# Six block numbers for each tile in one register load, and new durations for the queue planner, in a block-sparse attention and feed-forward kernel

## The chip, the cores and the metric

The kernel runs on one core of a Trainium2 chip. The metric is the time of one execution on the device, in microseconds (us); smaller is better. A core has TensorE (PE in the profile, its weight loads PEld), VectorE (DVE), ScalarE (ACT), GpSimd (POOL) and SyncE (SP), each with an instruction queue of its own that is worked off in order. All DMAs of this kernel are issued from SP's queue.

## The reference, cut to what matters

```python
# q, k, v: (4, 8, 768, 64); sampled_blocks: (24, 3); blocks of 32 positions
scores = scale * np.matmul(q, k.transpose(0, 1, 3, 2))
mask = np.abs(blk_i - blk_j) <= 1                      # the window
mask = mask | (blk_i == 0) | (blk_j == 0) | (blk_i == n_blocks - 1) | (blk_j == n_blocks - 1)
for qb in range(n_blocks):
    for kb in sampled_blocks[qb]:                      # three sampled blocks for each block row
        mask[qb*32:(qb+1)*32, kb*32:(kb+1)*32] = True
attn = softmax(np.where(mask, scores, -1e9))
x = np.matmul(attn, v).transpose(0, 2, 1, 3).reshape(3072, 512)
h = x @ w_in                                           # 512 -> 2048
return np.maximum(0.01 * h, h) @ w_out                 # 2048 -> 512
```

The sampled block numbers are an input, so the kernel learns only on the chip which blocks of K and V to fetch.

## The kernel before, in words

**Tiles.** A tile is two block rows (64 queries) of all eight heads of one of four batches. There are twelve tiles in a batch. Tile 0 holds the first and the last block row, which see all keys. The other eleven, T = 1 to 11, so 44 in all, see twelve blocks of keys, called slots: slots 0 to 3 are the window, 4 and 5 the first and last block, and 6 to 11 are the six sampled ones, three for each of the tile's two block rows. Each value is kept as two halves of 16 bits, so that matmuls run in f16.

**Gathering K.** `gather_k` fills one of two buffers `kg` with the twelve key blocks from the transposed keys `kt`: VectorE copies the window (and the edges once for a batch), and GpSimd copies the six sampled blocks, one copy each, in two tasks of three. **Gathering V.** `gather_v` fills one of two buffers `vg` by DMA from a scratch array `scr` in DRAM: one 128-row load for the window, two edge loads once for a batch and buffer, and six 32-row loads (moves) of sampled blocks, again in two tasks of three. A buffer of either kind comes free when the matmuls of the tile two before have read it.

**Block numbers.** `build_masks` clamps the sampled numbers, multiplies them by 32 and leaves them in the SBUF tile `offs`. `sampled_of` (line 982 of the profile) loads them into registers of the engine that needs them: GpSimd for the copies of K (line 1005), SP for the moves of V (line 1036). A call loads the three numbers of one half-task, so there are two calls for each tile on each of the two engines.

**After the gathers.** Scores (`s`) are matmuls of `kg` with the stacked queries `qs` and their half-swapped twin `qxs`; VectorE and ScalarE make the softmax (`p`, then the two halves `pp`); SP transposes `pp` into `pt` by DMA (in the first item, TensorE does); `pair_av` multiplies `pt` with `vg` in three chunks of four slots, in the order of the slots, so the last three sampled blocks are in its last chunk. Four tiles make an item; each item goes through the feed-forward layer (`h`, then `ht` and `g`, then `o`), whose matmuls are TensorE's other work. Weights are decoded, scaled and split during the first quarter of the run.

**What sets the order.** Every call on an engine is recorded as a task of a `Plan` (so most instructions have line 384 in the profile). `Plan.order` then runs a simulation with the durations of `cost`: each engine takes, among the tasks whose inputs are ready, the one of the lowest priority number, which follows the step (half a head pair of a tile) at which it was recorded or which it serves. TensorE also prefers to stay with matmuls of one kind. The order in which tasks begin in that simulation is the fixed order in which each engine's instructions are written. A task has `busy` (how long its engine is taken), `late` (when its result is there) and, for a DMA, `loads`: the transfers, which fly 1.25 us, share the DMA engines and are done 0.4 us after they were served. A task of SP with `loads` is only done, for tasks that need it, when its last load has landed. The half-tasks of the gathers do not go through `cost`; their durations are given where they are recorded:

```python
plan.task("POOL", copies, 2150.0, 2150.0, cells(kt) | cells(offs), cells(kg[:, :, at:at + NR * BLOCK]))
...
plan.task("SP", moves, 1850.0, 1850.0, cells(scr[b]) | cells(offs), into, "",
          [BLOCK * (9.3 + 0.055 * 2048) / 16] * NR)
```

The last arguments but the loads are what the task reads and writes, as sets of cells; a task that writes a cell comes after the one that wrote or read it before.

Of the kernel before, what the change touches and what calls it, by code (L numbers as in the profile page):

```python
# [16 lines left out]
I32 = mybir.dt.int32  # L17
# [15 lines left out]
    "ahead": 3,  # L33
    "av_lag": 3,
    "bs": 1500,
    "early": 2,
    "flag": 1,
    "g": 2,
    "g_at": 0,
# [348 lines left out]
def cost(eng, method, a, k):  # L388

    out = k.get("out", a[0] if a else None)  # L390
    n = elements(out)
    apply = lambda x: hasattr(x, "ap")
    if eng == "PE":
        lhs, rhs = a[1], a[2]
        cols = elements(rhs)
        if lhs.dtype == F32:
            return 60.0 + 4 * cols, 300.0 + 4 * cols, "f", []
        half = elements(lhs) <= 64
        t = (cols / 2.4 + 2.5) / CFG["clock"]
        return (t / 2 if half else t), t + 180, ("a" if half else "f"), []  # L400
    if eng == "SP" or method.startswith("dma"):
        turned = method == "dma_start_transpose"
        w = transfer(k["out"], k["in_"], turned)
        rows = len([d for d in list(k["out"].ap) if d[1] > 1])
        busy = 1050.0 + 0.37 * n if turned else 380.0 + 110 * max(0, rows - 1)
        return busy, busy, "", [w]
    if eng == "DVE":
        ptr = sum(1 for x in (k.get("scalar"), k.get("scalar1"), k.get("scale")) if apply(x)) > 0
        src = [x for m, x in k.items() if m in ("in0", "in1", "in_") and apply(x)]
        wide = [x for x in src if elements(x) > 1]  # L410
        f = 1.0
        if method in ("tensor_copy", "tensor_scalar") and len(wide) == 1 and wide[0].space == bass.MemoryType.SB:
            f = 0.5
            if method == "tensor_copy" and wide[0].dtype == F16 and out.dtype == F16:
                f = 0.25
        if method == "tensor_reduce":
            n = elements(k["in_"])
        d = 145 + 62 * ptr + n * f / 0.96
        if len(wide) == 2 and all(x.space == bass.MemoryType.SB for x in wide) and n >= 256:
            d *= 1.08  # L420
        acc = method == "tensor_tensor_reduce"
        return max(d - 70, 60.0), d + 12 + 80 * acc, "", []
    if eng == "ACT":
        src = a[1]
        ptr = any(apply(k.get(x)) for x in ("scale", "bias"))
        d = n * 0.833 + (155 if src.space == bass.MemoryType.PSUM else 187) + 93 * ptr
        acc = "accum_out" in k
        return d - 92 + 100 * acc, d + 14 + 93 * acc, "", []
    d = 120 + n * (2.2 if method == "tensor_tensor" else 1.3)
    return d + 20, d + 12, "", []  # L430
# [3 lines left out]
def tile_block_sparse_attention_ffn(  # L434
# [165 lines left out]
    iota = cst.tile([NB, NB], F32, name="iota")  # L600
    tmps = pf.tile([P, DM], F32, tag="ob", name="tmps", bufs=CFG["ob"])
    sb = tmps[:NB, :2 * NR].bitcast(I32)
    row = tmps[:1, 6:6 + 2 * NB * NR].bitcast(I32)
    eq = tmps[:NB, 150:150 + NR * NB].rearrange("p (r b) -> p r b", r=NR)
    sels = [tmps[:NB, 222 + P * a:222 + P * (a + 1)].rearrange("p (a b c) -> p a b c", a=2, b=2) for a in range(2)]
    assert 222 + 2 * P <= DM and 6 + 2 * NB * NR <= 150
    offs = cst.tile([1, NT - 1, 2, 4], I32, name="offs")
    mask = cst.tile([P, NT - 1, SLOTS], F32, name="mask")

    def load_constants():  # L610
        nc.sync.dma_start(out=eye, in_=c_eye)
        nc.vector.tensor_copy(out=eye16, in_=eye)
        nc.sync.dma_start(out=row, in_=sampled.bitcast(I32).rearrange("(o a) b -> o (a b)", o=1))
        nc.sync.dma_start(out=allow, in_=c_allow)
        nc.sync.dma_start(out=iota, in_=c_iota)
        nc.sync.dma_start(out=sb, in_=sampled.bitcast(I32))

    def build_masks():
        blocks = row.rearrange("p (a b) -> p a b", b=2)[:, NR:NR + (NT - 1) * 2 * NR, 0]
        nc.vector.memset(offs, 0)  # L620
        nc.vector.tensor_scalar(
            out=offs[:, :, :, :NR], in0=blocks.rearrange("p (t a r) -> p t a r", a=2, r=NR), scalar1=0, scalar2=NB - 1,
            op0=ALU.max, op1=ALU.min)
        nc.vector.tensor_scalar(out=offs, in0=offs, scalar1=5, scalar2=None, op0=ALU.logical_shift_left)
        sf = cst.tile([NB, NR], F32, name="sf")
        nc.vector.tensor_copy(out=sf, in_=sb.rearrange("p (a b) -> p a b", b=2)[:, :, 0])

        ok = cst.tile([NB, NR], F32, name="ok")
        hit = cst.tile([NB, NB], F32, name="hit")
        for r in range(NR):  # L630
            nc.vector.tensor_scalar(out=eq[:, r, :], in0=iota, scalar1=sf[:, r:r + 1], scalar2=None, op0=ALU.is_equal)
            nc.vector.tensor_tensor(out=hit, in0=eq[:, r, :], in1=allow, op=ALU.mult)
            nc.vector.tensor_reduce(out=ok[:, r:r + 1], in_=hit, op=ALU.add, axis=AX.X)
            nc.vector.tensor_tensor(out=allow, in0=allow, in1=eq[:, r, :], op=ALU.max)
        nc.vector.tensor_scalar(out=ok, in0=ok, scalar1=-1.0, scalar2=1.0, op0=ALU.mult, op1=ALU.add)

        at = cst.tile([NB, NT - 1, 2, NR], F32, name="at")
        nc.gpsimd.affine_select(
            out=at.rearrange("p t a r -> p (t a) r"), in_=ok.unsqueeze(1).to_broadcast([NB, NB - 2, NR]),
            pattern=[[-1, NB - 2], [0, NR]], base=-1, channel_multiplier=1,  # L640
            compare_op=ALU.is_equal, fill=0.0)
        pm = corner()[:, :(NT - 1) * 2 * NR].rearrange("p (t a r) -> p t a r", t=NT - 1, a=2)
        for a in range(2):
            sel = sels[a]
            nc.vector.memset(sel, 0.0)
            nc.vector.memset(sel[:, :, a, :], 1.0)
            nc.tensor.matmul(
                pm[:, :, a, :], sel.rearrange("p a b c -> p (a b c)"), at[:, :, a, :], start=True, stop=True)
        nc.vector.tensor_scalar(
            out=mask[:, :, 6:], in0=pm.rearrange("p t a r -> p t (a r)"), scalar1=-1.0, scalar2=-NEG,  # L650
            op0=ALU.add, op1=ALU.mult)
        nc.vector.memset(mask[:, :, :6], 0.0)
        for hh in range(2):
            a, b = (slice(D * hh + BLOCK * i, D * hh + BLOCK * (i + 1)) for i in range(2))
            nc.vector.memset(mask[a, :, 3:4], NEG)
            nc.vector.memset(mask[b, :, 0:1], NEG)
            nc.vector.memset(mask[a, 0:1, 4:5], NEG)
            nc.vector.memset(mask[b, NT - 2:NT - 1, 5:6], NEG)
# [318 lines left out]
    kgs, vgs = {}, {}  # L977
    last_use = {}

    def sampled_of(T, a, engine):  # L980

        _, rows = tc.nc.values_load_multi_w_load_instructions(
            offs.ap[:1, T - 1, a, :NR], engines={engine}, min_val=0, max_val=S - BLOCK,
            skip_runtime_bounds_check_because="the block numbers are clamped to the sequence before they are shifted")
        return zip(range(6 + a * NR, 6 + (a + 1) * NR), rows)

    kgb = [pa.tile([P, H, KEYS], F16, tag=f"kg{i}", name=f"kg{i}", bufs=1) for i in range(2)]
    ends = {}
# [1 line left out]
    def gather_k(b, T):  # L990
# [6 lines left out]
        if ends.get(n) != b:  # L997
            ends[n] = b
            nc.vector.tensor_copy(
                out=kg[:, :, P:P + Q2].rearrange("p h (n l) -> p h n l", l=BLOCK),  # L1000
                in_=kt.rearrange("p h (n l) -> p h n l", l=BLOCK)[:, :, 0:NB:NB - 1, :])
        for a in range(2):
            def copies(a=a):
                for slot, off in sampled_of(T, a, mybir.EngineType.Pool):
                    tc.nc.gpsimd.tensor_copy(  # L1005
                        out=kg.ap[:, :, slot * BLOCK:(slot + 1) * BLOCK], in_=kt.ap[:, :, bass.ds(off, BLOCK)])
            at = (6 + a * NR) * BLOCK
            plan.task("POOL", copies, 2150.0, 2150.0, cells(kt) | cells(offs), cells(kg[:, :, at:at + NR * BLOCK]))
            yield
        em = pa.tile([P, KEYS], BF16, tag="em", name=f"em_{b}_{T}", bufs=2)  # L1010
        nc.gpsimd.tensor_copy(
# [8 lines left out]
    def gather_v(b, T):  # L1020
# [6 lines left out]
        if vends.get(n) != b:  # L1027
            vends[n] = b
            for slot, a in ((4, 0), (5, S - BLOCK)):
                ps, c = place(slot)  # L1030
                nc.sync.dma_start(out=vg[ps, c, :], in_=scr[b][a:a + BLOCK, :])
        for a in range(2):
            def moves(a=a):
                for slot, off in sampled_of(T, a, mybir.EngineType.SP):
                    ps, c = place(slot)
                    tc.nc.sync.dma_start(out=vg.ap[ps, c, :], in_=scr[b].ap[bass.ds(off, BLOCK), :])
            into = set()
            for slot in range(6 + a * NR, 6 + (a + 1) * NR):
                ps, c = place(slot)
                into |= cells(vg[ps, c, :])  # L1040
            plan.task("SP", moves, 1850.0, 1850.0, cells(scr[b]) | cells(offs), into, "",
                      [BLOCK * (9.3 + 0.055 * 2048) / 16] * NR)
        vgs[b, T] = vg.rearrange("p c (h x) -> p c h x", h=H)

# [578 lines left out]
```

## Time and profile before

| | |
|---|---|
| median of three runs | 924.11 us (923.51 to 927.22) |
| the profiled execution: its time, its span | 927.57 us, 925.9 us |
| granted TensorE clock, mean over the span | 0.932 |
| busy: PE, DVE, ACT, POOL | 767.3, 626.3, 509.4, 330.0 us |
| instructions | 20826 |

Busy time is the time in which an engine worked on something; instructions of a queue itself (register loads, DMA issues, waits) are not counted in it and carry a q after the engine's name, as in SPq. A row of the list of waits says who was idle, for whom, how long in total, how many times, and the longest of these. A row of the view of one line or tile gives the count, then the least, median and greatest duration in ns.

### The profile page before, as it was taken

The numbers are of one execution on the slowest core, as the hardware profiler recorded it, in microseconds if no ns is written. First come the engines' busy times: TensorE is split into PE (matmuls) and PEld (weight loads), VectorE is DVE, ScalarE is ACT, GpSimd is POOL, SyncE is SP. The second block draws the span as 40 slices with busy tenths as digits, with TensorE's granted clock in tenths as the row PEclk, the third lists the DMA queues.
The fourth block names the chain that finished last, engine by engine and source line by source line (L and its number), as shares of the span: only waits on it lengthen the run. The fifth ranks groups of instructions, "written<-read, shape, count | busy, mean of one in ns | idle before, by whom it ended". The sixth has DMA issues, their size and how long they took to land. (4 is left out here: it accounts for less than half of the span.)

```text
span 925.9 us, 20826 instructions
## 1 busy us (share of the span) xinstructions
PE 767.3 (83%) x7204; PEld 499.0 (54%) x7204; DVE 626.3 (68%) x1650; ACT 509.4 (55%) x1087; POOL 330.0 (36%) x469
## 2 busy tenths in 40 slices
PE   2647566688889978988788988988898899999998
PEld 2425443444556645555554655655565555656664
DVE  4698789998979945856748657667467466474221
ACT  5678766556655635645546556556357355274121
POOL 0234356523324523433413433324314344242221
PEclk9566678888999999999999999999999999999999
DMA  9504896488797767798677878786765867466000
GB/s 182 201 18 124 256 237 171 115 197 166 149 169 168 169 133 153 155 175 160 138 169 132 169 148 161 177 155 138 166 146 123 161 125 156 89 133 125 1 23 24
DMA packets 312231, 133.29 MB, mean 144 GB/s; under 512 B 275005, under 2 KB 287294, under 8 KB 312126
## 3 DMA queue, kind: packets, MB, share of 16 engines
q1 hardware_dynamic: 312126, 131.96, 65.7%
q8 instruction: 57, 0.93, 0.4%
q14 instruction: 48, 0.39, 0.1%
HBM read 65.57 MB, written 12.58 MB: 84 GB/s over the span
## 5 line engine op out<-in xcount | busy, mean ns | idle before, releaser
L384 PEld LDWEIGHTS <-W 128*128 128x128 f16 (+1 forms) x2480 | 237.8, 101 | 83.6 <-DVE W L384 24.5
L384 PE MATMUL o<-W,g 128*128 128x512 f16 x1152 | 278.1, 388 | 4.0 <-DVE g L384 2.8
L384 PE MATMUL h<-x,W 128*128 128x256 f16 x2304 | 278.4, 276 | 3.0 <-ACT x L384 2.1
L384 POOL TENSOR_TENSOR g<-ht,g 128x512 f16<-128x512 f32 x96 | 117.1, 1220 | 285.0 <-DVE g L384 207.0
L384 PEld LDWEIGHTS <-g 128*128 128x128 f16 x1152 | 109.6, 100 | 132.5 <-issue 21.0
L384 DVE SCALAR_TENSOR_TENSOR pp<-p,r,pp 128x384 f16<-128x384 f32 x208 | 147.6, 738 | 45.6 <-ACT pp L384 45.1
L384 ACT ACTIVATE p<-p,mx 128x384 f32<-128x384 f32 x208 | 125.8, 606 | 91.9 <-DVE mx L384 91.2
L1005 POOL COPY kg<-kt 128x256 f16 x264 | 125.9, 515 | 138.5 <-PE s L384 113.7
L384 ACT ACTIVATE pp<-p,r 128x384 f16<-128x384 f32 x208 | 118.8, 606 | 75.4 <-DMA pt<-pp 26.8
L384 PE MATMUL av<-pt,vg 128*64 128x128 f16 x2112 | 90.5, 228 | 54.5 <-DMA vg<-scr 29.6
L384 DVE SCALAR_TENSOR_TENSOR ht<-h,gd,ht 128x512 f32<-128x512 f32 x80 | 59.9, 749 | 106.3 <-ACT ht L384 105.8
L384 DVE CUSTOM_DVE_ANT_0 p<-s,em,nsc 128x384 f32<-128x384 f32 x176 | 104.7, 609 | 31.6 <-PE s L384 30.6
L384 ACT ACTIVATE ht<-h,gs 128x512 f32<-128x512 f32 x80 | 54.5, 681 | 118.4 <-PE h L384 110.7
L384 PEld LDWEIGHTS <-vg 128*64 128x64 f16 x2112 | 71.8, 114 | 88.4 <-issue 70.2
L384 PE MATMUL s<-kg,qs 128*64 128x384 f16 x352 | 64.0, 354 | 15.9 <-DVE mx L384 14.0
L384 POOL TENSOR_TENSOR x<-xf,x 128x256 f16<-128x256 f32 x48 | 35.9, 747 | 96.2 <-ACT x L384 96.0
L384 PE MATMUL s<-kg,qxs 128*64 128x384 f16 x352 | 63.5, 349 | 4.7 <-DMA qxs<-qs 4.7
L384 PEld LDWEIGHTS <-qs 128*64 128x64 f16 x416 | 29.2, 114 | 40.9 <-issue 32.0
L384 DVE CAST g<-ht 128x512 f16<-128x512 f32 x96 | 42.5, 443 | 10.8 <-PE o L384 6.5
L384 ACT ACTIVATION_READ_ACCUMULATOR p<-p,mx 128x1 f32 x208 | 39.1, 188 | 0.0
L384 DVE TENSOR_SCALAR sum<-sum 128x2 f32<-128x2 f32 x96 | 28.5, 297 | 15.3 <-ACT p L384 14.7
L384 POOL TENSOR_TENSOR W<-W 128x1024 f16<-128x1024 f32 x12 | 28.1, 2349 | 27.9 <-ACT W L384 25.6
(117 smaller groups left out, 759.8 us busy)
## 6 DMA issues: line engine op xcount, KB each, us to landing
vg<-scr SPq DMA_DIRECT2D x280, 64.0 KB, 1.9
vg<-scr SPq DMA_DIRECT2D x44, 256.0 KB, 3.2
v<-in_v_dram SPq DMA_DIRECT2D x32, 192.0 KB, 4.2
qxs<-qs SPq DMA_DIRECT2D x48, 128.0 KB, 2.4
scr<-v SPq DMA_DIRECT2D x16, 384.0 KB, 3.3
rq<-in_q_dram SPq DMA_DIRECT2D x20, 256.0 KB, 3.9
W<-in_moe_w_in_dram SPq DMA_DIRECT2D x5, 1024.0 KB, 7.5
out_dram<-ob SPq DMA_DIRECT2D x20, 256.0 KB, 2.5
```

What stands on the lines that cost most here:

```text
L384: self.plan.task(self.eng, lambda: f(*a, **k), busy, late, reads, writes, kind, loads)
L1005: tc.nc.gpsimd.tensor_copy(out=kg.ap[:, :, slot * BLOCK:(slot + 1) * BLOCK], in_=kt.ap[:, :, bass.ds(off, BLOCK)])
```

## The change

One load of six numbers takes the place of two loads of three: the first half-task of a tile's gather loads all six registers of its engine, and the second uses the last three of them. `offs` holds eight words for a tile in one row instead of two rows of four. So that the registers are not overwritten in between, the half-tasks of K write a made-up cell `("registers",)` and those of V a made-up cell `("moves",)`, which puts all half-tasks of one kind in one chain, across tiles too.

The planner's durations change as well. A half-task of K was 2150 ns; it is now 560 for each of three copies, and 800 more in the first half for the load. A half-task of V was 1850 ns; it is now 560 for each of three moves, and 800 more in the first half. Every other DMA that is not a transpose is planned at 425 ns for its issue, and 110 more for each dimension beyond the first, where it was 380.

```diff
-    "early": 2,
+    "kcopy": 560.0, "load": 800.0, "vmove": 560.0, "early": 2,
...
-        busy = 1050.0 + 0.37 * n if turned else 380.0 + 110 * max(0, rows - 1)
+        busy = 1050.0 + 0.37 * n if turned else 425.0 + 110 * max(0, rows - 1)
...
-    offs = cst.tile([1, NT - 1, 2, 4], I32, name="offs")
+    offs = cst.tile([1, NT - 1, 8], I32, name="offs")
...
-    def sampled_of(T, a, engine):
+    def sampled_of(T, engine):
...
-            offs.ap[:1, T - 1, a, :NR], engines={engine}, min_val=0, max_val=S - BLOCK,
+            offs.ap[:1, T - 1, :2 * NR], engines={engine}, min_val=0, max_val=S - BLOCK,
...
-        return zip(range(6 + a * NR, 6 + (a + 1) * NR), rows)
+        return list(zip(range(6, SLOTS), rows))
...
+        found = []
         for a in range(2):
             def copies(a=a):
-                for slot, off in sampled_of(T, a, mybir.EngineType.Pool):
+                if not a:
+                    found.extend(sampled_of(T, mybir.EngineType.Pool))
+                for slot, off in found[a * NR:(a + 1) * NR]:
...
-            plan.task("POOL", copies, 2150.0, 2150.0, cells(kt) | cells(offs), cells(kg[:, :, at:at + NR * BLOCK]))
+            t = CFG["kcopy"] * NR + (0.0 if a else CFG["load"])
+            plan.task("POOL", copies, t, t, cells(kt) | cells(offs),
+                      cells(kg[:, :, at:at + NR * BLOCK]) | {("registers",)})
...
+        got = []
         for a in range(2):
             def moves(a=a):
-                for slot, off in sampled_of(T, a, mybir.EngineType.SP):
+                if not a:
+                    got.extend(sampled_of(T, mybir.EngineType.SP))
+                for slot, off in got[a * NR:(a + 1) * NR]:
...
-            into = set()
+            into = {("moves",)}
...
-            plan.task("SP", moves, 1850.0, 1850.0, cells(scr[b]) | cells(offs), into, "",
+            t = CFG["vmove"] * NR + (0.0 if a else CFG["load"])
+            plan.task("SP", moves, t, t, cells(scr[b]) | cells(offs), into, "",
                       [BLOCK * (9.3 + 0.055 * 2048) / 16] * NR)
```

More of the change, by code (lines that the diff above doesn't have):

```diff
@@ L602, in tile_block_sparse_attention_ffn @@
     sb = tmps[:NB, :2 * NR].bitcast(I32)
-    row = tmps[:1, 6:6 + 2 * NB * NR].bitcast(I32)
+    rows = tmps[:1, 6:6 + 2 * NB * NR].bitcast(I32)
     eq = tmps[:NB, 150:150 + NR * NB].rearrange("p (r b) -> p r b", r=NR)
@@ L612, in load_constants @@
         nc.vector.tensor_copy(out=eye16, in_=eye)
-        nc.sync.dma_start(out=row, in_=sampled.bitcast(I32).rearrange("(o a) b -> o (a b)", o=1))
+        nc.sync.dma_start(out=rows, in_=sampled.bitcast(I32).rearrange("(o a) b -> o (a b)", o=1))
         nc.sync.dma_start(out=allow, in_=c_allow)
@@ L618, in build_masks @@
     def build_masks():
-        blocks = row.rearrange("p (a b) -> p a b", b=2)[:, NR:NR + (NT - 1) * 2 * NR, 0]
+        of_tile = rows.rearrange("p (a b) -> p a b", b=2)[:, NR:NR + (NT - 1) * 2 * NR, 0].rearrange(
+            "p (t a) -> p t a", a=2 * NR)
         nc.vector.memset(offs, 0)
         nc.vector.tensor_scalar(
-            out=offs[:, :, :, :NR], in0=blocks.rearrange("p (t a r) -> p t a r", a=2, r=NR), scalar1=0, scalar2=NB - 1,
-            op0=ALU.max, op1=ALU.min)
+            out=offs[:, :, :2 * NR], in0=of_tile[:1], scalar1=0, scalar2=NB - 1, op0=ALU.max, op1=ALU.min)
         nc.vector.tensor_scalar(out=offs, in0=offs, scalar1=5, scalar2=None, op0=ALU.logical_shift_left)
```

## The prediction

> **What bounds the kernel now.** I read the page's busy times first, then the stages by windows, TensorE's waits in the stage that has most of them, and last SP's queue around one gather. TensorE is the busiest engine by far, and its clock is nearly full after the first quarter:
>
> ```profile
> PE 767.3 (83%) x7204; PEld 499.0 (54%) x7204; DVE 626.3 (68%) x1650; ACT 509.4 (55%) x1087; POOL 330.0 (36%) x469
> PEclk9566678888999999999999999999999999999999
> ```
>
> By stages (time in the window, then each engine's busy time and count, the granted clock, the DMA engines' share):
>
> ```profile
> core 0: us, PE busy (x) PEld busy (x) DVE busy (x) ACT busy (x) POOL busy (x), PEclk, DMA share, GB/s
> 0.00:85.00 85.00, 43.81 (x360) 30.91 (x360) 59.96 (x193) 59.25 (x107) 18.63 (x32) 0.70 0.50 126
> 85.00:250.00 165.00, 121.47 (x1130) 79.82 (x1130) 148.72 (x353) 108.82 (x211) 76.21 (x84) 0.81 0.74 185
> 700.00:850.00 150.00, 138.52 (x1384) 89.88 (x1381) 90.95 (x240) 77.39 (x181) 59.10 (x91) 0.99 0.64 132
> 250.00:700.00 450.00, 391.60 (x3811) 250.33 (x3812) 309.19 (x837) 250.14 (x572) 159.81 (x250) 0.99 0.77 157
> ```
>
> The last row is a window of its own for the middle of the run. TensorE idles 41 us in the first 85, 44 us up to 250, 58.4 us from 250 to 700 (450 less 391.60), and 11.5 us from 700 to 850. Up to 250 VectorE is the limit (148.72 of 165 busy: weights are prepared there), and no gather is on the path. In the middle stage these are the waits, against the only large one of the stage from 700 to 850 (last row, of a second answer):
>
> ```profile
> PE av L384 <- DMA vg<-scr: 29.6, 20, 2.7
> PE av L384 <- DMA pt<-pp: 14.0, 17, 1.7
> PE s L384 <- DMA qxs<-qs: 4.4, 4, 1.4
> PE s L384 <- DVE mx L384: 4.1, 5, 2.2
> ...
> PE av L384 <- DMA pt<-pp: 10.4, 10, 2.3
> ```
>
> Half of TensorE's idle time in the middle, 29.6 of 58.4 us, is `av` waiting for V's gather: 20 waits of 1.48 us in the mean, all of these before 700. The rest is mostly transposes that SP issues too. So what SP issues for V and when, and where the plan puts `av` against it, is where this change can act. One wait seen close, SP's rows and then TensorE's (start, length, count; a register load has no row of its own here, and fills the time ahead of the L1036 rows):
>
> ```profile
> 565.98 0.49 SPq L384 DMA_DIRECT2D vg<-scr  x1
> 567.46 1.45 SPq L1036 DMA_DIRECT2D vg<-scr  x3
> 569.01 1.26 SPq L384 DMA_TRANSPOSE pt<-pp  x1
> 571.60 1.34 SPq L1036 DMA_DIRECT2D vg<-scr  x3
> ...
> 572.69 0.41 PE L384 MATMUL av<-pt,vg 128*64 128x128 f16 x8
> 574.43 0.64 PE L384 MATMUL av<-pt,vg 128*64 128x128 f16 x16 [1.33 <-DMA vg<-scr]
> ```
>
> Eight matmuls, two chunks of slots, run; the third chunk is the last three blocks, issued until 572.94, and TensorE waits 1.33 us for them. TensorE's place for `av` was fixed by the plan, which had V there sooner.
>
> **The change part by part.** *The loads themselves.* These rows have the register loads of both queues, what SP does for one move (three rows of L1036), and the other DMAs in play:
>
> ```profile
> L982 POOLq TENSOR_LOAD <-offs x88: 724/740/2223, 26.6 to 820.3; - x88
> L982 SPq TENSOR_LOAD <-offs x88: 664/690/1141, 83.5 to 845.2; - x88
> L1036 SPq FUSED_REGOPS  x147: 37/37/47, 250.2 to 694.8; - x147
> L1036 SPq MOVE vg<-scr x147: 29/29/38, 250.2 to 694.9; - x147
> L1036 SPq DMA_DIRECT2D vg<-scr x147: 315/316/1650, 250.3 to 695.0; - x147
> DMA to landing us min/median/max: 1.7/1.8/3.6
> L384 SPq DMA_DIRECT2D vg<-scr x60: 332/526/1662, 82.1 to 842.1; - x60
> L384 SPq DMA_DIRECT2D qxs<-qs x48: 467/582/1060, 18.6 to 819.3; - x48
> L384 SPq DMA_TRANSPOSE pt<-pp x188: 1209/1238/3180, 127.5 to 853.6; - x188
> ```
>
> Each queue loses 44 of its 88 loads, and each of the other 44 fetches six numbers. No row shows a load of six. If it costs what one of three costs, 0.690 us, SP saves 0.690 for each tile, 30 us of queue time in all; if it goes by the number of values, 1.380 us, it saves nothing. I take 1.34: a queue step that touches no memory takes 0.037 (FUSED_REGOPS), so 0.653 of the 0.690 is fetching, far above any such step, which looks more like three trips of 0.218 than like one; 0.037 + 6 x 0.218 = 1.34. The saving is then 2 x 0.690 - 1.34 = 0.04 us for each tile, under 2 us in 44 tiles: nothing.
> The Trainium skill, page "Runtime: NRT & Kernel Launch", section "Instruction fetch mechanics", speaks against the change here: it states that a register load costs about 200 ns for each register, even for many at once. By that page three would be 0.6 us, which the trace's 0.690 does not contradict, and six an estimated 1.29 (0.69 + 0.6), a saving of 0.09 us for each tile and 4 us of SP's queue in all; no run here has another count to try it on.
>
> *What the plan thinks of V.* This is the term I count on. With both halves back to back the gather looks like this:
>
> ```profile
> 445.00 1.66 SPq L384 DMA_DIRECT2D vg<-scr  x1
> 447.65 3.60 SPq L1036 DMA_DIRECT2D vg<-scr  x6
> 451.35 1.25 SPq L384 DMA_TRANSPOSE pt<-pp  x1
> ```
>
> From the end of the window's load (446.66) to the last move's end (451.25) are 4.59 us, both register loads included; the plan had 2 x 1.85 = 3.70, so V is 0.89 us later than planned, before anything that lands late. After the change it is 4.59 less 2 x 0.69 plus 1.34, so 4.55, and the plan has 2.48 + 1.68 = 4.16: 0.39 late. The plan gets 0.50 us nearer (with a load at 0.690, 3.90 against 4.16: 1.15 us nearer; at 1.380, 0.46 nearer). The fixed order then puts `av` that much later against V, and TensorE does `h` or `o` in between: 20 waits x 0.50 = 10 us of the 29.6.
> Not all is kept, for the transposes are late next. With no wait for V, the stage from 700 to 850 has 10.4 us of waits for `pt` in 150, so 31 in 450, where the middle stage has 14.0: had all 29.6 gone, 17 would come back and 42% be kept. By its whole idle time, 11.5 in 150 or 34.5 in 450 against 58.4, 24 of 29.6 or 81% would be kept. Between them I take 60%: 6 us. The ends are 0 (all comes back) and 24 us (the middle as good as the stage after it).
>
> *The chain of half-tasks.* In the plan V's second half now starts only after the first has landed, so something else of SP's queue goes between. Often that is so already (the transpose between the two halves at 569.01), and a transpose of 1.24 us is one that the plan knows and prices. I count nothing for it, between minus 1.24 us in a tile whose halves lay together (the second half is late by a transpose) and some gain (the plan delays `av` as well). It is the place of the slow rival below. Across tiles the chain adds nothing: the tile before has landed long ago.
>
> *K.* On GpSimd 0.74 becomes at most 1.48 ahead of the first three copies, and nothing ahead of the second. I cost that at nothing, since the queue fetches registers while the engine waits for the buffer, and since `s` waits for no copy of K in the middle stage:
>
> ```profile
> POOL kg L1005 <- PE s L384: 113.7, 30, 8.8
> PE o L384 <- POOL g L384: 1.0, 2, 0.7
> ```
>
> Were that cover gone, 44 x 0.74 = 33 us of GpSimd would lie ahead of K and of what is queued behind it, the splits `g` and `x`; `o` waits for `g` 1.0 us in the whole run, and GpSimd is busy 159.81 of 450. In the plan a tile's K goes from 4.30 to 4.16, hardly a move.
>
> *Other DMAs.* 425 for 380, and 110 for a second dimension: 0.535 where it was 0.490, against 0.526 and 0.582 in the rows above. Nothing gets faster; the order may change anywhere, from the first load on, and by the rows I can give that no sign. In `build_masks` the same instructions run on as many words: nothing.
>
> *Sum.* 6 us from V, the rest nothing. Against the profiled execution (927.57 us, its span 925.9 and 1.7 around it) that is 921.6; that execution lies 3.5 above the median of 924.11, so against the median 918.
>
> **The rivals.** *First, the load is one trip.* At 0.690 SP's queue gets 0.690 us for each tile and V's lateness falls by 1.15 us: 20 x 1.15 = 23 us, 60% of it 14: 910. For it: the numbers lie side by side in one row. Against it: 0.690 is long for one trip beside the 0.037 of a register step.
>
> *Second, all comes back.* The plan's nearer V moves `av` later, but `av` then waits for `pt`, or SP's order, shuffled by the 45 ns on each DMA, loses elsewhere what it wins here. For it: `pt` waits 10.4 us in the one stage without waits for V. It gives 924. That the change does little (a load by values, K hidden) is in here too.
>
> *Third, slower: V's second half caught behind a blocked step.* SP works in order. If what goes between the halves is a step that itself must wait, the second half sits behind it. How long such steps wait in the middle stage:
>
> ```profile
> SPq L384 <- PE s L384: 28.3, 31, 2.4
> SPq L384 <- PE av L384: 21.8, 23, 2.2
> ```
>
> The mean is 0.91 and 0.95. With 147 / 6 = 24 tiles in the stage, 24 x 0.93 = 22 us that the plan doesn't see, 60% of it 13, less the 6 won: 931. It decides once half the tiles (12 x 0.93 x 0.6 = 6.7) are hit. For it: every tile now has such a gap, and the last chunk, which waits, is the one behind it. Against it: many tiles have the gap now, and the step between is mostly a transpose.
>
> **How the numbers follow.** A difference under 0.5%, 4.6 us here, can't be told from no change. Chances: the forecast 0.36 (918, its own range 911 to 923), the load in one trip 0.20 (910, down to 900 with the 24 us of the upper end), all back 0.20 (924), slower 0.24 (931, up to 937 without the 6 won). The range of 904 to 933 leaves out about one in ten on each side. Faster by over 0.5%, below 919.5: 0.32 of the forecast's 0.36 and all of the first rival's 0.20, so 0.52; slower, above 928.7: the third rival's 0.24; within: 0.24.
>
> **What would show it.** Register loads at 44 on each queue; their median near 1.3 us, not 0.7. Waits of `av` for `vg` in the middle fall from 29.6 to about 20 us, at most 1 us each in most cases, and those for `pt` rise from 14. K shows no wait of `s` on GpSimd. I am wrong if the load's median is 0.7 (then it should be near 910), if the waits for `vg` stay or grow (the third rival, with SP's waits between the two halves), or if the idle time before 250 changes by more than a few us, which none of these terms explains.

## The result, and the profile after

The changed kernel took 889.39 us (median of four, 885.38 to 891.25) against 924.79 us of the kernel before beside it: a ratio of 0.9609, 95% interval 0.9568 to 0.9649. That is 3.9% faster, 35 us, where 918 was forecast and 904 was the low end.

The profiled execution took 888.39 us, its span 886.7. The page's lines of the span and of the busy times, then four stages by windows (columns as before):

```profile
span 886.7 us, 20717 instructions
PE 761.0 (86%) x7204; PEld 498.0 (56%) x7204; DVE 615.6 (69%) x1650; ACT 507.1 (57%) x1087; POOL 336.3 (38%) x469
```

```profile
0.00:85.00 85.00, 44.59 (x365) 31.61 (x366) 61.71 (x197) 60.76 (x111) 19.98 (x35) 0.82 0.50 129
85.00:250.00 165.00, 118.90 (x1122) 81.00 (x1122) 143.37 (x348) 106.72 (x205) 74.53 (x80) 0.78 0.79 186
250.00:700.00 450.00, 420.78 (x4160) 269.38 (x4159) 324.57 (x890) 268.37 (x617) 184.09 (x276) 1.00 0.83 167
700.00:850.00 150.00, 144.78 (x1357) 95.93 (x1356) 78.91 (x205) 66.19 (x150) 50.79 (x73) 0.99 0.50 108
```

TensorE's idle time in the whole span fell from 158.6 to 125.7 us (span less busy), and its busy time by 6.3. In the first two stages the idle time is as it was (84.7 before, 86.5 now). In the middle it halved, 58.4 to 29.2, and from 700 to 850 it went from 11.5 to 5.2. The middle runs more matmuls in the same 450 us: 4160 for 3811.

TensorE's waits in the middle stage, longest in total first, and the first row of the stage from 700 to 850:

```profile
PE av L384 <- DMA vg<-scr: 11.5, 9, 2.5
PE s L384 <- DVE mx L384: 4.4, 6, 1.6
PE av L384 <- DMA pt<-pp: 4.0, 5, 1.2
...
PE av L384 <- DMA vg<-scr: 3.0, 3, 1.3
```

Waits for V in this stage went from 29.6 us to 11.5, and those for the transposes fell too, from 14.0 to 4.0: they did not come back as the next wait. Over the whole run the waits for V fell less, from 29.6 to 19.6 us, for a single wait of 5.1 us now lies between 85 and 250. The register loads, and SP's queue around one gather:

```profile
L982 POOLq TENSOR_LOAD <-offs x44: 773/829/1963, 28.7 to 776.9; - x44
L982 SPq TENSOR_LOAD <-offs x44: 720/744/1389, 81.6 to 800.1; - x44
```

```profile
348.01 0.52 SPq L384 DMA_DIRECT2D vg<-scr  x1
349.57 1.43 SPq L1044 DMA_DIRECT2D vg<-scr  x3
351.10 2.58 SPq L384 DMA_TRANSPOSE pt<-pp  x2
353.72 0.58 SPq L384 DMA_DIRECT2D rq<-in_q_dram  x1
354.83 1.34 SPq L1044 DMA_DIRECT2D vg<-scr  x3
```

Six numbers cost 0.744 us where three cost 0.690, not 1.34. By medians SP spends 44 x 0.744 = 33 us on loads instead of 88 x 0.690 = 61: 28 us less. The median hides the long ones: added up over each trace, the loads take 69.8 us before and 37.0 after, 33 us less. The load stands between 348.53 and 349.57; nothing is fetched ahead of the second half, and other steps of the queue lie between the two.

### The profile page after: what moved, and what is told of

Its sections match the earlier page's. It is cut to its first block, busy times and chain, and to the rows that moved or that the text cites. A ratio compares the mean times of both kernels' runs of the same rounds, so it can differ in the third digit from the quotient of the medians.

```text
span 886.7 us, 20717 instructions
## 1 busy us (share of the span) xinstructions
PE 761.0 (86%) x7204; PEld 498.0 (56%) x7204; DVE 615.6 (69%) x1650; ACT 507.1 (57%) x1087; POOL 336.3 (38%) x469
## 5 line engine op out<-in xcount | busy, mean ns | idle before, releaser
L384 PE MATMUL h<-x,W 128*128 128x256 f16 x2304 | 281.4, 277 | 13.4 <-ACT x L384 8.4
L384 PE MATMUL o<-W,g 128*128 128x512 f16 x1152 | 272.8, 382 | 0.0
L384 DVE SCALAR_TENSOR_TENSOR pp<-p,r,pp 128x384 f16<-128x384 f32 x208 | 139.9, 699 | 43.0 <-ACT pp L384 42.4
L1008 POOL COPY kg<-kt 128x256 f16 x264 | 129.3, 528 | 86.4 <-PE s L384 74.4
L384 ACT ACTIVATE pp<-p,r 128x384 f16<-128x384 f32 x208 | 119.0, 606 | 59.9 <-DMA pt<-pp 28.8
L384 PE MATMUL av<-pt,vg 128*64 128x128 f16 x2112 | 84.3, 228 | 25.5 <-DMA vg<-scr 19.6
L384 PEld LDWEIGHTS <-vg 128*64 128x64 f16 x2112 | 69.0, 114 | 51.4 <-issue 37.9
L384 PE MATMUL s<-kg,qs 128*64 128x384 f16 x352 | 64.1, 358 | 21.7 <-DVE mx L384 20.1
L384 POOL TENSOR_TENSOR x<-xf,x 128x256 f16<-128x256 f32 x48 | 38.0, 791 | 96.8 <-ACT x L384 96.7
L384 DVE TENSOR_SCALAR sum<-sum 128x2 f32<-128x2 f32 x96 | 29.2, 305 | 10.7 <-ACT p L384 10.1
```

The lines of the kernel that those rows point to most:

```text
L384: self.plan.task(self.eng, lambda: f(*a, **k), busy, late, reads, writes, kind, loads)
L1008: tc.nc.gpsimd.tensor_copy(out=kg.ap[:, :, slot * BLOCK:(slot + 1) * BLOCK], in_=kt.ap[:, :, bass.ds(off, BLOCK)])
```

## The experiments

Two theories stood at first. L: the time of the saved loads is the gain. O: the new order is. All medians below are of four runs unless told; ratios are against the kernel before, beside them on the same chip.

### The load, in either order

The changed order with the loads of before:

```diff
-                if not a:
-                    got.extend(sampled_of(T, mybir.EngineType.SP))
-                for slot, off in got[a * NR:(a + 1) * NR]:
+                for slot, off in sampled_of(T, mybir.EngineType.SP, a):   # three numbers; the same for K
```

> The changed kernel's order on every engine, but each half-task fetches its own three numbers again, on SP and GpSimd: 88 loads on each queue, and nothing else differs. Theory L (the saved load is the gain: six numbers cost 0.744 us where three cost 0.690, so SP's queue gets 0.64 us back for each tile, 28 us in all): 910 to 917, most of the 35 us given back. Theory O (the new order is the gain, the load only frees a queue that has slack): 889 to 896. Both together: 898 to 908.

It took 911.99 us, 0.9834 (0.9788 to 0.9880). And the old order with one load of six (the changed kernel with 380, 1850 and 2150 ns again and without the two made-up cells):

> The order of the kernel before on every engine, with one load of six where it had two of three: 44 loads on each queue. Theory L: 898 to 908, most of the gain. Theory O: 918 to 925, since the fixed order of the other engines stays as planned. In both, the waits of av for vg in the middle (29.6 us) should fall by up to 20 x 0.64 = 13 us, as each gather's last block is issued 0.64 us earlier.

It took 898.73 us, 0.9680 (0.9631 to 0.9729). So by medians the loads bring 26 us in the old order (924.8 to 898.7) and 22.6 in the new one (912.0 to 889.4); the order brings 9 to 13. By the ratios, each of which has an interval of some 4 us to either side, it is 30 and 21 us for the loads and 7 to 15 for the order (differences of the ratios, times 925 us). Both theories have a share, and L the larger. TensorE's waits in the whole run, the transposes before (first row), then both in the old order with one load:

```profile
PE av L384 <- DMA pt<-pp: 25.0, 29, 2.3
...
PE av L384 <- DMA pt<-pp: 17.8, 24, 2.1
PE av L384 <- DMA vg<-scr: 12.4, 16, 1.6
```

With the order kept, the waits for V are 17 us down from 29.6, and those for the transposes 7.

### Which queue

The changed order with two loads of three on SP alone, then on GpSimd alone:

> The changed kernel's order, with two loads of three on SP alone; GpSimd keeps one of six. Theory SPQ (SP's queue is what the middle stage runs on, so its 28 us come back nearly whole): 908 to 913, all of the 22 us that two loads on both queues cost. Theory K (GpSimd's loads lie on a path, by the copies of K or the splits behind them): under 898.

> The changed kernel's order, with two loads of three on GpSimd alone; SP keeps one of six. Theory SPQ: 887 to 892, no change. Theory K: 900 to 911.

914.06 us (0.9868, 0.9834 to 0.9902) and 887.92 us (0.9598, 0.9558 to 0.9638). The register loads of the first kernel and its middle stage by windows, then the same of the second:

```profile
L983 SPq TENSOR_LOAD <-offs x88: 666/714/1748, 80.9 to 828.8; - x88
L983 POOLq TENSOR_LOAD <-offs x44: 774/848/1687, 28.5 to 802.4; - x44
```

```profile
250.00:700.00 450.00, 403.14 (x3946) 258.22 (x3946) 309.82 (x860) 258.03 (x589) 174.22 (x265) 0.99 0.80 159
```

```profile
L983 POOLq TENSOR_LOAD <-offs x88: 725/752/2030, 28.6 to 779.6; - x88
L983 SPq TENSOR_LOAD <-offs x44: 722/740/1223, 81.9 to 800.6; - x44
```

```profile
250.00:700.00 450.00, 422.75 (x4168) 270.54 (x4166) 323.80 (x892) 269.56 (x619) 185.46 (x276) 1.00 0.84 167
```

In this order all of it is SP's: 44 more loads on GpSimd change nothing that the intervals show, and 44 more on SP take 18 us of TensorE's middle stage (420.78 to 403.14 busy in 450).

### What a load costs

Fetching for three tiles at once should take SP's queue still less:

```diff
-    offs = cst.tile([1, NT - 1, 8], I32, name="offs")
+    offs = cst.tile([1, (NT - 1) * 8], I32, name="offs")   # six words for each tile, close together
...
+        if (T - 1) % 3 == 0:                                # 18 numbers (12 for the last two tiles)
```

> The changed kernel's order, with one load of 18 numbers on each queue for three tiles (16 loads on each queue instead of 44). From 0.690 for three and 0.744 for six, 18 values should cost about 0.96 us: SP's queue would lose 44 x 0.744 = 33 us of loads and get 16 x 0.96 = 15 back, so 17 us less. Theory SPQ, with some 80% of saved queue time seen in the end: 873 to 878. If a load goes by single values beyond some count, or SP has slack by now: 887 to 892.

It was slower than one load for each tile and outside both ranges: 895.08 us, 0.9650 (0.9618 to 0.9681). SP's 16 loads add up to 39.0 us there, more than the 37.0 of the changed kernel's 44. Four loads of SP in a row, those of one batch:

```profile
L987 SPq TENSOR_LOAD <-offs x1: 1412/1412/1412, 312.9 to 312.9; - x1
L987 SPq TENSOR_LOAD <-offs x1: 3735/3735/3735, 348.2 to 348.2; - x1
L987 SPq TENSOR_LOAD <-offs x1: 1618/1618/1618, 398.2 to 398.2; - x1
L987 SPq TENSOR_LOAD <-offs x1: 2498/2498/2498, 437.6 to 437.6; - x1
```

The first three fetch 18 numbers, the last 12. The second and the fourth start 72 and 216 bytes into `offs`, 8 bytes past a multiple of 16, and cost 0.208 us for each number; the first and third start on one and cost less than half. That suggested theory Q: four numbers on a 16-byte step come in one trip, and any other number takes a trip by itself. As worded it does not cover the second load, for behind its first two numbers four others start on such a step and still cost 0.208 each; counted in fours from the load's own first number, each a single trip only if it starts on a step, it does. Three tests of it. All eight words of a tile's row, two unused (`offs.ap[:1, T - 1, :]` for `offs.ap[:1, T - 1, :2 * NR]`):

> The changed kernel in the same order; each load fetches all eight words of a tile's row of offs, two of them unused. Loads so far: 0.664 us at least for three numbers; 0.720 for six at the start of a row of eight words; 2.50 for 12 and 3.7 for 18 that start 8 bytes off a 16-byte step (0.208 each); 1.41 to 1.62 for 18 that start on one. Theory Q (four numbers that start on a 16-byte step come in one trip of 0.25 to 0.30, any other number singly at 0.208): eight cost 0.55 to 0.60, less than six; SP gets 0.15 x 44 = 7 us back: 882 to 887. Theory V (a load grows by some 0.02 for each number): 0.78, and 888 to 892.

Twelve numbers for two tiles, in rows of 16 words (`offs = cst.tile([1, 6, 16], I32)`, a load when T is odd):

> The changed kernel's order; one load of 12 numbers for two tiles (24 loads on each queue, four of them of six), in rows of 16 words so that each starts on a 64-byte step. Theory Q: 0.80 to 0.90 for 12, all loads of SP some 20 us instead of 37, and 17 us less of SP's queue, of which some 80% is seen: 874 to 880. Theory V with a price by length that bends somewhere between 6 and 18: 1.2 or more, 887 to 893.

And in the kernel before, with the same instructions in the same order, four words instead of three (`offs.ap[:1, T - 1, a, :]` for `offs.ap[:1, T - 1, a, :NR]`):

> The kernel before, the same instructions in the same order on every engine, with 88 loads on each queue as before; each load fetches all four words of a row of offs instead of three of them. By theory Q (one trip of some 0.21 us for four aligned numbers or for a single one, and about 0.1 around it) a load takes 0.30 to 0.35 us instead of 0.690, and SP gets 88 x 0.36 = 32 us back, as much as the change gives it: 895 to 901, like the old order with one load of six (898.7). If the number of loads counts and not their time: 922 to 927.

SP's loads of the three:

```profile
L982 SPq TENSOR_LOAD <-offs x44: 525/546/1169, 81.7 to 799.6; - x44
```

```profile
L991 SPq TENSOR_LOAD <-offs x24: 736/769/1384, 80.5 to 790.4; - x24
```

```profile
L982 SPq TENSOR_LOAD <-offs x88: 295/311/777, 82.8 to 820.3; - x88
```

Four numbers cost 0.311 us, eight 0.546, twelve 0.769, against 0.690 for three and 0.744 for six. An estimate of 0.22 for a trip and 0.08 around it comes within 0.05 us of all five, with one trip of four for the first, then two and three of four, three single ones, and one of four with two single. Theory V, by the number of values, is out: eight cost less than six, and four less than half of three.

What stands ahead of a load counts too. These are the two of the gather that the prediction shows from 565.98 on, the first behind the window's load of V, the second behind the transpose at 569.01:

```profile
L982 SPq TENSOR_LOAD <-offs x1: 684/684/684, 566.5 to 566.5; - x1
L982 SPq TENSOR_LOAD <-offs x1: 1088/1088/1088, 570.3 to 570.3; - x1
```

In the kernel before, 18 of SP's 88 loads stand right behind such a transpose, with a median of 1.06 us, where the 56 behind a load of `vg` have 0.68. With one load for each tile, at the head of its gather, the changed kernel has 6 behind a transpose; its order with two loads has 26. That is one more reason why the sums differ from the medians.

In time: loads of four gave 901.58 us, 0.9744 (0.9705 to 0.9782), against the 924.7 beside it. The old program with one more word fetched by each load, and as many loads, gains 23 us, nearly what one load of six gained in that order. It is the time of the loads that counts, not their number. (This run shortens GpSimd's loads as well; that SP's alone count was tried only in the new order.) The old kernel fetched three words of a padded row of four, at twice the price of all four. Two tiles at once gave 877.45 us, 0.9486 (0.9437 to 0.9536), the best so far and clear of the changed kernel: SP's loads are 24 x 0.769 = 18 us there. Loads of eight gave 888.32 us, 0.9602 (0.9553 to 0.9651): 9 us less of loads and nothing seen. The price came as theory Q had it, the time missed its 882 to 887, and the interval, down to 884, does not exclude the upper part of that.

### The order

Three edits make the new plan: the new durations of half-tasks, the chain, and 425 ns for other DMAs. With one load of six in all of them, these were run: without the 425 ns, without the chain, without the new halves, and each of the three alone.

> The changed kernel with only the planned issue of other DMAs put back to 380 ns. If the gain lies in the gathers (their planned halves, their chain, the load): 886 to 895. If it needs the 45 ns on each other DMA: 905 to 920. A reordering without a cause of its own would show as 885 to 905, either side.

> The changed kernel without the two made-up cells, so that in the plan a second half may follow its first at once and need not wait for its landing; one load of six is kept. If the chain brings the gain, by making the plan put V later: 905 to 920, with waits of av for vg back at 25 to 35 us. If the planned durations of the halves or the load bring it: 886 to 895.

> The changed kernel with the planned half-tasks put back to 2150 (K) and 1850 (V) each; the chain, the 425 ns and one load of six are kept. If the truer durations of V bring the part of the gain that the load does not (about 10 us): 896 to 902. If any new order would do, or the chain and the 425 ns do it: 886 to 893.

> One load of six in a plan with the old 380 ns and without the chain, but with the new durations of the half-tasks (K 2480 and 1680, V 2480 and 1680). The old plan with one load took 898.7, the new one 889. If V's truer durations bring the ten us: 887 to 892. If any two of the three edits to the plan are needed: 895 to 901.

> One load of six in a plan with the old 380 ns and the old durations of the half-tasks, but with the chain of half-tasks. If the truer durations bring the ten us: 896 to 901. If the chain does, or any reordering: 887 to 892.

> One load of six in a plan with the old half-tasks and without the chain, but with 425 ns for other DMAs. Plans so far with one load: old 898.7, new halves alone 905.4, chain alone 890.4, chain with either other edit 889 to 892, halves with 425 but no chain 890.5. If the 425 ns can bring the ten us alone too: 887 to 893. If not (then it needs the chain or a pair): 896 to 903.

| plan, with one load of six | us | ratio, 95% interval |
|---|---|---|
| none of the three edits | 898.73 | 0.9680 (0.9631 to 0.9729) |
| halves alone | 905.39 | 0.9787 (0.9732 to 0.9843) |
| 425 alone | 900.87 | 0.9730 (0.9689 to 0.9772) |
| chain alone | 890.36 | 0.9622 (0.9572 to 0.9671) |
| halves and 425 | 890.53 | 0.9591 (0.9540 to 0.9641) |
| halves and chain | 889.44 | 0.9605 (0.9559 to 0.9652) |
| 425 and chain | 891.65 | 0.9621 (0.9581 to 0.9661) |
| all three | 889.39 | 0.9609 (0.9568 to 0.9649) |

The truer durations of the half-tasks, K's and V's, alone made the order slower, if anything (905.39 was outside both expected ranges), so they are not what the order gains. Every plan with the chain is near 890, and so is one without it. The chain seems enough here, though its interval alone overlaps that of no edit, and it is not needed. The profile does not say why, for the waits of `av` do not follow the time: in the whole run they were 12.4 us for `vg` and 17.8 for `pt` with none of the edits, 9.9 and 11.9 with the halves alone, which was no faster, and 18.8 and 20.1 with the chain alone. What makes some orders ten us better than others stays open.

### Is it SP's queue as such?

If SP's queue paces the run, other work taken off it should help too. ScalarE issues the 32 writes of the output, at the same place in the plan (`tc.nc.scalar.dma_start` for `nc.sync.dma_start`); then the same on top of the load for two tiles:

> The changed kernel's plan and order; the 32 writes of the output (15 us of SP's queue) are issued by ScalarE, at the place that the plan gave them. Theory SPQ (whatever leaves SP's queue counts): 878 to 884. If only the time of the gathers counts, or ScalarE pays for the issues: 888 to 896.

> The aligned load of 12 numbers for two tiles (877.5 alone) and the output's writes issued by ScalarE. If both save queue time that still counts: 866 to 873. If SP's queue has slack by then: 876 to 880.

890.83 us (0.9630, 0.9588 to 0.9672) and 876.46 us (0.9498, 0.9456 to 0.9539): nothing either time, though 14 us (32 issues of 0.423, their median) left SP. ScalarE's issues took 0.356 each; whether it gave the gain away cannot be told from this. So idle time was put onto SP at two places instead, two small DMAs at a time:

```diff
+        for i in range(2):
+            tc.nc.sync.dma_start(out=sink[sunk[0]:sunk[0] + 1, :], in_=offs.ap[:1, 0, :])
+            sunk[0] += 1
```

> The changed kernel's order with two more DMAs of 32 bytes (offs to a place in DRAM that nobody reads) on SP right behind the first transpose of pp of each tile: 88 issues of some 0.37 us, 0.74 us for each of 44 tiles, as much as the second register load took. If SP's time counts wherever TensorE's next work is queued behind it: 905 to 916. If only the gather's own start counts: 889 to 896.

> The same 88 small DMAs, in pairs, behind 24 of the output's writes and 20 of the loads of q instead. If SP's queue paces the run as such: the same as beside the transposes, 905 to 916. If the writes and loads lie in slack that SP has (as e14 suggests): 889 to 897.

(There, e14 is the run with the writes of the output on ScalarE alone.)

Beside the transposes it took 918.17 us (nine runs; 0.9918, 0.9883 to 0.9952), beside the writes and loads of q 906.14 us (0.9785, 0.9728 to 0.9842): 29 us and 17 us lost. The row of the small DMAs and the middle stage by windows, first beside the transposes, then beside the writes:

```profile
L1149 SPq DMA_DIRECT2D sink<-offs x88: 211/336/576, 123.3 to 831.4; - x88
```

```profile
250.00:700.00 450.00, 404.61 (x3935) 257.57 (x3930) 311.35 (x858) 259.44 (x590) 174.92 (x264) 0.99 0.80 159
```

```profile
L1148 SPq DMA_DIRECT2D sink<-offs x88: 214/280/1018, 10.7 to 901.7; - x88
```

```profile
250.00:700.00 450.00, 408.52 (x4019) 261.21 (x4018) 315.51 (x874) 261.77 (x599) 177.00 (x268) 0.99 0.81 161
```

The small DMAs add up to 31 us in the first trace and 30 in the second (the medians hide some long ones), and the register loads grew with them, from 37.0 us to 44.3 and 39.9. So SP had some 38 us more to do at the transposes, of which 29 were paid in the run, and 33 us at the other place, of which 17 were paid; there 4 us of the small DMAs lie ahead of the first gather or behind the last one (10.7 to 901.7). So the start of the gather is not all that counts: time added to SP's queue while tiles run is paid for about half or more in the run. What the transfers of these DMAs themselves cost was not tried apart from their issues.

That less of it did not help with the writes, nor measurably with the loads of eight, has a sign in the traces. Added up over the whole run, SP's own records without its semaphore instructions take 610 us in the changed kernel. With the writes gone they take 606, not 594, and with loads of eight 607, not 601: other issues became longer by a good part of what was saved. Where the time moved by over ten us the sum moved with it: 592 with the load for two tiles, 646 and 645 with two loads of three on both queues or on SP alone, 650 and 637 with the small DMAs. These are sums of one trace each, and the load for two tiles with the writes on ScalarE has 581 and no gain over 592, so SP's queue is not all of it. Why other issues lengthen stays open.

## Why the prediction was wrong

*Where the time could come from* was right: the middle stage, TensorE waiting for what SP issues. In that stage the waits for V fell further than to the forecast 20 us, to 11.5.

*The price of a load* is the first step that failed. The sum took 1.34 us for six numbers, because 0.653 of a load of three "looks more like three trips of 0.218 than like one". Three trips fit the later loads; but six numbers are not six trips, as four of them come in one: 0.744. The traces have 0.208 for each number in a load that starts off a 16-byte step and 0.064 in the load of twelve that starts on one. The Trainium skill, page "Runtime: NRT & Kernel Launch", section "Instruction fetch mechanics", states about 200 ns for each register, even for many at once. Here the measurement decides. The median was named as what would show it, with "near 910" for 0.7.

*What the time is worth* is the second, and the larger one. With 0.690 the first rival came to 910: 20 waits x 1.15 us, 60% kept, 14 us, and the load's own part of that, 0.69 of the 1.15, is 8 us. The load alone was worth 22 to 26 us by medians. The sum priced only the waits that TensorE shows for V. But the loads left SP's queue in all 44 tiles: 28 us by medians, 36 us added up over the traces in the old order and 40 in the new one, and more than half of that came back as run time. The transposes stand in the same queue and were earlier too. "All comes back", and the 40% taken off for it, had that the wrong way round: waits for `pt` were to rise from 14 us and fell to 4.0, and with the load alone, in the old order, from 25.0 to 17.8. That a wait for V stands in for the next wait on the same queue is the reading that fits; no run shows a single wait passed on.

*The plan nearer to the truth* was the term of 6 us that the forecast stood on. The order did bring 9 to 13 us, but not by this mechanism: with the truer durations alone it took 905.4 against 898.7, though the waits for V did fall, 12.4 to 9.9 us. The term had about the size, by luck, and the wrong cause. The 4.16 us that it takes for the new plan also holds only if the halves lie back to back; the chain puts the first half's landing between them, over a microsecond by the planner's own durations, so the plan itself moved further than the 0.50 us. Counting nothing for the chain and the 45 ns held for each of them taken away from the changed plan (890.5, 889.4), and seems not to hold for the chain put alone into the old one (890.4 against 898.7, with intervals that overlap).

*K at nothing* was right: two loads on GpSimd gave 887.92. *The slow rival* did not come: the plan without the chain took 890.53, the one with it 889.39.

*The range* reached down to 904, and its best case was 910 ("down to 900") with a chance of 0.20. A sign against it was in the trace before: added up, SP's own records, again without its semaphore instructions, take 386 of the middle stage's 450 us, while the argument looked at TensorE's waits and never summed SP's queue. It also called the rest of the idle time there "mostly transposes"; they are 14.0 of 28.8 us.

## What to carry to other kernels

When the waits of the busiest engine all lead to one issuing queue, price a saved step by the time that it takes on that queue, in every tile, and not by the waits that name it: the waits are shared by all that the queue issues. Take that time as an upper bound: here more than half of it came back for the register loads, and nothing for the writes or the loads of eight. Add the rows up, too, where a few are much longer than the median. A register load of block numbers cost by trips here, so pad the row to a multiple of four words on a 16-byte step and fetch the padding too, or the numbers of two tiles at once. A new order of a planner has a spread of its own that nothing here explained, some 16 us between plans with the same instructions to run, so keep the instructions and the order apart when one change has both: the same loads in the old order and the old loads in the new one took two runs.

## What the runs showed that was not expected

- A register load of four numbers takes 0.311 us and one of three 0.690; eight take 0.546 and six 0.744.
- A load of 18 numbers took 1.41 us from one start and 3.74 from another, 8 bytes off a 16-byte step.
- The same load of three took 0.68 us at the median behind a load of `vg` and 1.06 right behind a DMA transpose.
- 31 us of small DMAs that nobody waits for, on SP beside the transposes, cost the run 29 us and made the register loads 7 us longer.
